# Copies of q's and k's parts spread over nine slots, and P's transposes ranked ninety places ahead

## The chip, the cores and the metric

The kernel runs on one core of a Trainium2 chip. The core has five engines with an instruction stream each: TensorE (PE in the rows, with its weight loads as PEld), VectorE (DVE), ScalarE (ACT), GpSimd (POOL) and SyncE (SP), which here only issues DMAs. The metric is the device time of one execution in microseconds (us); lower is better.

## The reference

Thresholded attention feeds two gated feed-forward blocks. What is computed, cut to what matters:

```python
# q, k, v: 4 batches x 8 heads x 576 rows x 64, float32
scores = (1 / np.sqrt(64)) * np.matmul(q, k.transpose(0, 1, 3, 2))
thresh = np.max(scores, axis=-1, keepdims=True) - tau
scores = np.where(scores >= thresh, scores, -1000000000.0)
attn = np.exp(scores - np.max(scores, axis=-1, keepdims=True))
attn = attn / (np.sum(attn, axis=-1, keepdims=True) + 1e-09)
x = np.matmul(attn, v)                      # to 2304 tokens x 512
x = (1 / (1 + np.exp(-(x @ w_gate)))) * (x @ w_val) @ w_out    # d_ff 1536
x = ((x @ w1) * (x @ w2)) @ w3 @ w_out2                        # d_ff 1024
```

## The kernel before, in words

**Three stretches.** Attention runs first, and the first block's matmuls (and, at the start, the product of w3 and w_out2) are put between attention's instructions as filler for TensorE, by `filler` and `budget`. At some 680 us attention is over, and the rest of the first block and the second block follow.

**Slots.** Attention is 16 pairs of heads (`NPAIR` = 4 for each of 4 batches), and a pair is 9 slots: four chunks of 128 query rows for each of two heads, and one slot for both heads' 64 last rows. That makes 144 slots, numbered 0 to 143 here; slot g is pair g // 9. The main loop runs over g. For a slot:

- `s_mm` (L295) makes a 128 x 576 block of scores in PSUM, as products of `qa` with `ka` and `ylz`. Two PSUM tiles take turns, so the scores of slot g + 2 wait until the mask of slot g has read its own.
- `s_max` (L317) takes the maximum on DVE, `s_exp` (L324) the exponentials on ACT into one of four `e` tiles, and `s_mask` (L331) masks on DVE.
- `s_hi` and `s_lo` (L341, L348) cut P, scaled, into a high and a low float16 part, in one of four `h16` tiles (`h` in the rows): the high part on ACT, the low part on POOL or DVE.
- `s_tr` (L362) transposes both parts with one DMA into one of five `pt` tiles. It is written two slots behind `s_mm`'s own slot.
- `pv` (L367) multiplies `pt` with V's parts on TensorE. It is written five slots behind (`LAG`).

So there are three rings: an `e` tile is free again after `s_lo`, an `h16` tile after its transpose has landed, a `pt` tile after `pv`.

**A pair's preparation.** While pair n runs, the table `ahead` places the steps that prepare pair n + 1 by slot: q's chunks are transposed on TensorE (`q_pe`), cut into a high part `xq` and a low part `yq` (`q_act`, `q_dve`), and the same for k (`xk`, `yk`). `dup` (L201) then stacks for each head `xq` over `yq` in `qa`, and `xk` over `xk` in `ka`, four SBUF to SBUF copies a head, because TensorE contracts over 128 partitions and a head has 64; `low` (L214) copies a half of `yk` into `ylz`. The loads of q, k and v for pair n + 2 stand in the same table.

**What sets the order.** Each engine runs its instructions in order. The order is set when the kernel is built, by a scheduler that takes instructions as they become ready in its own timeline, by priority; priority is the place in the program, and `tc.high_priority(offset=RING)` moves what is inside it 90 places ahead (`RING` = 90). In the kernel before, the next slots' scores, maximum, exponentials and the mask stand inside such a block. All DMAs of the kernel, the weights' loads and stores too, are issued by SP, one after the other; SP's list is therefore a queue in which an issue stands behind all issues ahead of it.

Of the kernel before, what the change touches and what calls it, by code (L numbers as in the profile page):

```python
# [8 lines left out]
F32 = mybir.dt.float32  # L9
F32R = mybir.dt.float32r  # L10
# [12 lines left out]
def kernel(  # L23
# [22 lines left out]
    nc = tc.nc  # L46
    P = 128
# [150 lines left out]
                op0=ALU.mult, op1=ALU.subtract,  # L198
            )

    def dup(pr, h):  # L201

        p = prep[pr]
        xq, yq, xk = (p[n].bitcast(F32) for n in ("xq", "yq", "xk"))
        qa = ap_.tile([P, NM], F32R, tag=f"qa{h}", name="qa", bufs=2)
        nc.sync.dma_start(qa[hsl[h]].bitcast(F32), xq[hsl[h]])
        nc.sync.dma_start(qa[hsl[1 - h]].bitcast(F32), yq[hsl[h]])
        ka = ap_.tile([P, S], F32R, tag=f"ka{h}", name="ka", bufs=2)
        for sl in hsl:
            nc.sync.dma_start(ka[sl].bitcast(F32), xk[hsl[h]])  # L210
        p.setdefault("qa", []).append(qa)
        p.setdefault("ka", []).append(ka)

    def low(pr, h):  # L214

        nc.sync.dma_start(ylz[h][hsl[h]].bitcast(F32), prep[pr]["yk"][hsl[h]].bitcast(F32))

    def low0(pr):
        low(pr, 0)

    def low1(pr):
        low(pr, 1)

    def dup0(pr):
        dup(pr, 0)

    def dup1(pr):
        dup(pr, 1)

    def k_pe(pr):  # L230
        prep[pr]["kps"] = transposed("k")
# [585 lines left out]
    l1 = None  # L817
    next(merge)
    t_pe(0, 0)
    for step in (q_pe, q_act, q_dve, k_pe, k_act, k_dve, dup0, low0, dup1, low1):  # L820
        step(0)
    load(q, 1, "q")
    load(k, 1, "k")
# [1 line left out]

    ahead = {
        0: ([], [], [], [t_pe], [q_pe]),
        1: ([q_act], [q_dve], [], [], []),
        2: ([], [v_max], ["q"], [], [k_pe]),
        3: ([k_act], [k_dve], [], [v_pe1], []),  # L830
        4: ([], [v_scale], [dup0, low0, dup1, "k"], [], []),
        5: ([], [], [], [v_pe2], []),
        6: ([], [v_mul], [], [], []),
        7: ([v_split], [], [], [], []),
        8: ([], [], [low1, "v"], [], []),
    }
# [28 lines left out]
    for g in range(G + LAG + 3):  # L865
        pr, s = divmod(g, NSL)
        steps = ahead[s] if pr + 1 < NP else ([],) * 5
        done = divmod(g - LAG, NSL)
        with tc.high_priority(offset=RING):
            if g < G:  # L870
                s_mask(g)
            if g + 1 < G:
                s_max(g + 1)
                s_exp(g + 1)
            if g + 2 < G:
                s_mm(g + 2)
        if g < G:
            s_hi(g)
        for f in steps[3]:
            f(pr + 1, g)  # L880
        if done[1] == 0 and done[0] > 0:
            x_norm(done[0] - 1)
        if g < G and g % 2 == 0 or g // (NPAIR * NSL) == 0:
            s_lo(g)
        if 0 < g <= G and not ((g - 1) % 2 == 0 or (g - 1) // (NPAIR * NSL) == 0):
            s_lo(g - 1)
        if 2 <= g < G + 2:
            s_tr(g - 2)
        for f in steps[0]:
            f(pr + 1)  # L890
        for f in steps[1]:
            f(pr + 1)
        if done[1] == 2 and done[0] > 0:
            x_act(done[0] - 1)
            if done[0] % NPAIR == 0:
                xdone[0] = done[0] // NPAIR
        filler(g, 0)
        for f in steps[2]:
            if isinstance(f, str):
                if pr + 2 < NP:  # L900
                    load(src[f], pr + 2, f)
            else:
                f(pr + 1)
        if 0 <= g - LAG < G:
            pv(g - LAG, g)
        for f in steps[4]:
            f(pr + 1)
        if done[1] == 1 and done[0] > 0:
            x_pe(done[0] - 1, g)
        filler(g, 1)  # L910
# [270 lines left out]
```

## Time and profile before

| | |
|---|---|
| median of 3 runs | 1116.5 us (1116.19 to 1119.25) |
| span of the profiled execution | 1115.6 us |
| TensorE busy | 1008.3 us, 90% of the span |
| VectorE busy | 774.8 us, 69% |
| GpSimd busy | 676.3 us, 61% |
| ScalarE busy | 627.6 us, 56% |

The profile gives the profiled execution's time as the span from its first to its last instruction, 1115.6 us, 0.9 us below the median of the runs. Busy shares are means over the three stretches, which have different limits. A wait is put down to what ended it.

### The profile page before, as it was taken

The numbers are of one execution on the slowest core, as the hardware profiler recorded it, in microseconds if no ns is written. First come the engines' busy times: TensorE is split into PE (matmuls) and PEld (weight loads), VectorE is DVE, ScalarE is ACT, GpSimd is POOL, SyncE is SP. The second block draws the span as 40 slices with busy tenths as digits, with TensorE's granted clock in tenths as the row PEclk, the third lists the DMA queues.
The fourth block names the chain that finished last, engine by engine and source line by source line (L and its number), as shares of the span: only waits on it lengthen the run. The fifth ranks groups of instructions, "written<-read, shape, count | busy, mean of one in ns | idle before, by whom it ended". The sixth has DMA issues, their size and how long they took to land. (4 is left out here: it accounts for less than half of the span.)

```text
span 1115.6 us, 20323 instructions
## 1 busy us (share of the span) xinstructions
PE 1008.3 (90%) x6960; PEld 884.9 (79%) x6960; DVE 774.8 (69%) x1380; ACT 627.6 (56%) x1245; POOL 676.3 (61%) x577
## 2 busy tenths in 40 slices
PE   2598956898987999999999998999999999999997
PEld 2477845676765787777877888999999989988996
DVE  6978687888897767767877645776767644652741
ACT  4868898767777676567667644554442322331321
POOL 3755475587888586678677855677664643462530
PEclk9789967999988999999999999999999999999999
DMA  8999999999999999898988864677558826844922
GB/s 227 245 274 211 225 218 173 241 280 264 270 286 235 200 209 210 211 210 180 201 198 184 161 140 153 215 234 250 184 193 293 256 80 229 282 131 128 325 69 63
DMA packets 322422, 232.57 MB, mean 208 GB/s; under 512 B 225296, under 2 KB 253968, under 8 KB 322320
## 3 DMA queue, kind: packets, MB, share of 16 engines
q1 hardware_dynamic: 322320, 231.28, 80.9%
q8 instruction: 55, 0.90, 0.3%
q14 instruction: 47, 0.39, 0.1%
HBM read 133.17 MB, written 30.93 MB: 147 GB/s over the span
## 5 line engine op out<-in xcount | busy, mean ns | idle before, releaser
L358 POOL TENSOR_TENSOR h<-e,h 128x576 f16<-128x576 f32 x90 | 120.1, 1336 | 39.9 <-ACT e L355 29.7
L327 ACT ACTIVATE e<-ps_s,nm 128x576 f32<-128x576 f32 x144 | 106.1, 737 | 51.0 <-DVE nm L321 49.8
L336 DVE SCALAR_TENSOR_TENSOR e<-ps_s,th,e 128x576 f32<-128x576 f32 x144 | 116.2, 811 | 20.3 <-ACT th L328 12.5
L63 PEld LDWEIGHTS <-pt 128*128 128x128 f16 x2240 | 82.1, 101 | 58.8 <-DMA pt<-h 32.3
L321 DVE TENSOR_REDUCE nm<-ps_s 128x1 f32<-128x576 f32 x144 | 106.3, 751 | 28.9 <-PE ps_s L63 19.9
L344 ACT ACTIVATE h<-e 128x576 f16<-128x576 f32 x144 | 97.0, 678 | 28.3 <-DVE e L336 14.8
L63 PE MATMUL ps_s<-ka,qa 128*128 128x288 f32 x256 | 67.5, 351 | 42.2 <-DVE e L336 31.4
L63 PE MATMUL ps_h<-xl,gh 128*128 128x512 f32 (+1 forms) x240 | 94.7, 395 | 6.3 <-POOL xl L469 2.8
L63 PE MATMUL ps_h<-xl,vh 128*128 128x512 f32 (+1 forms) x240 | 92.7, 386 | 2.4 <-ACT th L685 1.3
L63 PE MATMUL ps_h<-xh,gl 128*128 128x512 f32 (+1 forms) x240 | 91.3, 380 | 3.3 <-POOL gl L469 3.3
L469 POOL TENSOR_TENSOR gl<-wg,gh 128x512 fp32r<-128x512 f32 x42 | 55.4, 1319 | 61.4 <-ACT gh L468 61.4
L63 PE MATMUL ps_y<-wm,abh 128*128 128x512 f32 x288 | 91.6, 390 | 0.2 <-DVE wm L469 0.2
L63 PE MATMUL ps_h<-xh,vl 128*128 128x512 f32 (+1 forms) x240 | 90.2, 376 | 1.6 <-POOL vl L469 1.6
L63 PE MATMUL ps_o<-gvl,oh 128*128 128x512 f32 (+1 forms) x240 | 90.4, 376 | 1.0 <-DVE XR L718 1.0
L63 PE MATMUL ps_h<-xh,gh 128*128 128x512 f32 (+1 forms) x240 | 90.8, 378 | 0.0
L63 PE MATMUL ps_h<-xh,vh 128*128 128x512 f32 (+1 forms) x240 | 90.2, 376 | 0.0
L63 PE MATMUL ps_o<-gvh,ol 128*128 128x512 f32 (+1 forms) x240 | 88.5, 369 | 0.3 <-POOL ol L469 0.3
L63 PE MATMUL ps_o<-gvh,oh 128*128 128x512 f32 (+1 forms) x240 | 88.2, 368 | 0.0
L63 PE MATMUL u<-vh,pt 128*128 128x64 f16 x640 | 62.6, 200 | 27.6 <-DMA pt<-h 27.2
L63 PEld LDWEIGHTS ps_s<-ka,qa 128*128 128x128 f32 x256 | 45.6, 210 | 50.5 <-DVE e L336 36.5
L360 DVE SCALAR_TENSOR_TENSOR h<-e,h 128x576 f16<-128x576 f32 x54 | 61.4, 1137 | 23.2 <-ACT h L344 22.8
L469 POOL TENSOR_TENSOR ol<-wo,oh 128x512 fp32r<-128x512 f32 x42 | 55.7, 1330 | 24.0 <-ACT oh L468 23.9
(198 smaller groups left out, 3025.2 us busy)
## 6 DMA issues: line engine op xcount, KB each, us to landing
wc<-sc_c SPq DMA_DIRECT2D x168, 256.0 KB, 3.2
sc_c<-wc SPq DMA_DIRECT2D x56, 256.0 KB, 2.9
XR<-in_moe_w_out_dram SPq DMA_DIRECT2D x20, 512.0 KB, 5.0
ka<-xk SPq DMA_DIRECT2D x64, 144.0 KB, 3.3
wg<-sc_g SPq DMA_DIRECT2D x36, 256.0 KB, 3.1
wv<-sc_v SPq DMA_DIRECT2D x36, 256.0 KB, 3.1
wo<-sc_o SPq DMA_DIRECT2D x36, 256.0 KB, 3.2
XR<-in_moe_w_dram SPq DMA_DIRECT2D x16, 512.0 KB, 5.0
```

Of the source, the lines that this page charges most:

```text
L63: nc.tensor.matmul(out_, lhsT, rhs, start=first, stop=last)
L321: nc.vector.tensor_reduce(nm, x["ps"], axis=AX.X, op=ALU.max, negate=True)
L327: nc.scalar.activation(e, x["ps"], AF.Exp, bias=x["nm"])
L336: nc.vector.scalar_tensor_tensor(x["e"], x["ps"], x["th"], x["e"], op0=ALU.is_ge, op1=ALU.mult, accum_out=prep[pr]["sum"][:, s:s + 1],)
L344: nc.scalar.activation(x["h16"][:, 0:S], x["e"], AF.Copy, scale=PSC)
L358: nc.gpsimd.tensor_tensor(lo, e, hi, op=ALU.subtract)
L360: nc.vector.scalar_tensor_tensor(lo, e, PSC, hi, op0=ALU.mult, op1=ALU.subtract)
L469: (lo_eng or nc.gpsimd).tensor_tensor(lo, x, hi.bitcast(F32), op=ALU.subtract)
```

## The change

`dup` becomes two steps, one for q and one for k, so that the copies of a pair stand in slots 2, 3, 4 and 5 instead of three quarters of them in slot 4; the copies themselves are the same. q's load moves from slot 2 to slot 1, k's from slot 4 to slot 6. And `s_tr` moves into a block of high priority, 90 places ahead of its place in the program.

```diff
-    def dup(pr, h):
-        p = prep[pr]
-        xq, yq, xk = (p[n].bitcast(F32) for n in ("xq", "yq", "xk"))
+    def dup_q(pr, h):
+        p = prep[pr]
         qa = ap_.tile([P, NM], F32R, tag=f"qa{h}", name="qa", bufs=2)
-        nc.sync.dma_start(qa[hsl[h]].bitcast(F32), xq[hsl[h]])
-        nc.sync.dma_start(qa[hsl[1 - h]].bitcast(F32), yq[hsl[h]])
+        for sl, n in ((hsl[h], "xq"), (hsl[1 - h], "yq")):
+            nc.sync.dma_start(qa[sl].bitcast(F32), p[n].bitcast(F32)[hsl[h]])
+        p.setdefault("qa", []).append(qa)
+
+    def dup_k(pr, h):
+        p = prep[pr]
         ka = ap_.tile([P, S], F32R, tag=f"ka{h}", name="ka", bufs=2)
         for sl in hsl:
-            nc.sync.dma_start(ka[sl].bitcast(F32), xk[hsl[h]])
+            nc.sync.dma_start(ka[sl].bitcast(F32), p["xk"].bitcast(F32)[hsl[h]])
...
     ahead = {
         0: ([], [], [], [t_pe], [q_pe]),
-        1: ([q_act], [q_dve], [], [], []),
-        2: ([], [v_max], ["q"], [], [k_pe]),
-        3: ([k_act], [k_dve], [], [v_pe1], []),
-        4: ([], [v_scale], [dup0, low0, dup1, "k"], [], []),
-        5: ([], [], [], [v_pe2], []),
-        6: ([], [v_mul], [], [], []),
+        1: ([q_act], [q_dve], ["q"], [], []),
+        2: ([], [v_max], [dupq0], [], [k_pe]),
+        3: ([k_act], [k_dve], [dupq1], [v_pe1], []),
+        4: ([], [v_scale], [dupk0], [], []),
+        5: ([], [], [low0, dupk1], [v_pe2], []),
+        6: ([], [v_mul], ["k"], [], []),
         7: ([v_split], [], [], [], []),
         8: ([], [], [low1, "v"], [], []),
     }
...
         if 2 <= g < G + 2:
-            s_tr(g - 2)
+            with tc.high_priority(offset=RING):
+                s_tr(g - 2)
```

The scheduler then sets another order on every engine. Three places show it. In the rows a line number is that of the kernel they come from: s_tr's DMA is L364 before and L358 of the change, the copies are L206, L207, L210 and L216 before and L205, L212 and L217 of the change, L440 and L434 load raw weights, L639 and L633 store cast ones.

SP's list up to the transpose of slot 57 (pt<-h_3745), before:

```order
L206 DMA qa<-xq 64x512
L207 DMA qa<-yq 64x512
L210 DMA ka<-xk 64x576 x2
L216 DMA ylz_95<-yk 64x576
L206 DMA qa<-xq 64x512
L207 DMA qa<-yq 64x512
L210 DMA ka<-xk 64x576 x2
L145 DMA km<-in_k_dram 128x4x64 x2
L149 DMA tails<-in_k_dram 64x2x64
L639 DMA sc_o_130<-wo 128x512
L440 DMA XR<-in_moe_w_gate_dram 128x4x128
L364 DMA_TRANSPOSE pt<-h_3745 128x9x128
```

SP's list around the transpose of slot 57 (pt<-h_3748), of the change:

```order
L205 DMA qa<-xq 64x512
L205 DMA qa<-yq 64x512
L633 DMA sc_o_129<-wo 128x512
L434 DMA XR<-in_moe_w_gate_dram 128x4x128
L205 DMA qa<-xq 64x512
L205 DMA qa<-yq 64x512
L358 DMA_TRANSPOSE pt<-h_3748 128x9x128
L633 DMA sc_g_107<-wg 128x512
L434 DMA XR<-in_moe_w_val_dram 128x4x128
L633 DMA sc_v_119<-wv 128x512
L434 DMA XR<-in_moe_w_out_dram 128x512
L212 DMA ka<-xk 64x576 x2
```

Of the twelve issues of the preparation that stood in one row ahead of this transpose, four are left ahead of it, the copies of qa; ka, ylz and k's load now stand behind it, and six issues of weights that stood ahead do too.

SP's list from the transpose of slot 24 (pt<-h_1850) to that of slot 25 (pt<-h_1888), before:

```order
L364 DMA_TRANSPOSE pt<-h_1850 128x9x128
L216 DMA ylz_96<-yk 64x576
L135 DMA vnat<-in_v_dram 64x2x64
L440 DMA XR<-in_moe_w_val_dram 128x4x128
L145 DMA vnat<-in_v_dram 128x256
L639 DMA sc_g_100<-wg 128x512
L145 DMA vnat<-in_v_dram 128x256
L149 DMA vnat<-in_v_dram 64x2x64
L364 DMA_TRANSPOSE pt<-h_1888 128x9x128
```

The last twelve rows up to the transpose of slot 25 in SP's list, of the change (five more rows stand between them and the transpose of slot 24):

```order
L282 DMA vsh<-vh 64x2x256
L434 DMA XR<-in_moe_w_out_dram 128x512
L283 DMA vsh<-vh 64x2x256
L135 DMA vnat<-in_v_dram 64x2x64
L145 DMA vnat<-in_v_dram 128x256 x2
L633 DMA sc_v_112<-wv 128x512
L149 DMA vnat<-in_v_dram 64x2x64
L145 DMA qm<-in_q_dram 128x4x64
L205 DMA qa<-xq 64x512
L205 DMA qa<-yq 64x512
L205 DMA qa<-xq 64x512
L358 DMA_TRANSPOSE pt<-h_1888 128x9x128
```

The transpose of slot 25 had seven issues between it and the one before it, and now has seventeen, three copies of qa among them.

TensorE's list up to the first rows of pv of slot 50, before; the rows with ka are the first half of the scores of slot 58:

```order
L156 MATMUL ps_t<-ident,km 128x128 x4
L63 MATMUL ps_h<-xl,vh 128x512
L63 MATMUL ps_s_88<-ka,qa 128x288 x2
L63 MATMUL ps_h<-xh,vl 128x512
L63 MATMUL ps_h<-xh,vh 128x512
L63 MATMUL ps_h<-xl,vh 128x512
L63 MATMUL ps_h<-xh,vl 128x512
L63 MATMUL ps_h<-xh,vh 128x512
L63 LDWEIGHTS pt
L63 MATMUL u<-vh,pt 128x64
```

TensorE's list at the end of pv of slot 49 and the start of pv of slot 50, of the change; the rows with ka and ylz are the scores of slot 54:

```order
L63 LDWEIGHTS pt
L63 MATMUL u<-vsh,pt 128x64
L63 MATMUL ps_s_88<-ka,qa 128x288 x2
L63 LDWEIGHTS pt
L63 MATMUL u<-vsh,pt 128x64
L63 LDWEIGHTS pt
L63 MATMUL u<-vh,pt 128x64
L63 MATMUL ps_s_88<-ylz_95,qa 128x288 x2
```

pv of slot 50 stood behind the scores' start of slot 58, and now stands behind that of slot 54: TensorE's list holds fewer matmuls between a slot's scores and its pv. Between the last score product of slot 50 and pv of slot 50 the list holds 108 matmuls of 512 columns, 32 of 288, 112 of 64 and 16 of 128 before, and 54, 16, 90 and 7 in the change.

## Rows read from the trace of the kernel before

**Rows 1.** Windows: stretch and its us, busy us of each engine, clock, DMA share, GB/s.

```profile
core 0: us, PE busy (x) PEld busy (x) DVE busy (x) ACT busy (x) POOL busy (x), PEclk, DMA share, GB/s
37.00:200.00 163.00, 128.31 (x1115) 108.73 (x1115) 130.26 (x260) 127.94 (x252) 94.41 (x76) 0.84 1.00 222
200.00:400.00 200.00, 173.94 (x1335) 142.00 (x1336) 170.28 (x314) 146.88 (x290) 149.59 (x122) 0.94 1.06 253
400.00:690.00 290.00, 277.84 (x2208) 226.80 (x2207) 201.07 (x369) 186.18 (x372) 201.50 (x171) 0.99 0.83 185
690.00:1116.00 426.00, 418.38 (x2270) 399.74 (x2268) 246.37 (x381) 145.65 (x293) 217.00 (x190) 1.00 0.60 196
```

**Rows 2.** Waits from 37 to 200 us: us in total, times, longest.

```profile
PE u L63 <- DMA pt<-h: 23.8, 15, 4.3
```

**Rows 3.** Waits from 200 to 400 us.

```profile
PE ps_s L63 <- DVE e L336: 11.1, 5, 5.2
...
ACT h L344 <- DMA pt<-h: 6.7, 7, 2.1
...
PE ps_h L63 <- POOL gl L469: 3.3, 2, 2.0
```

**Rows 4.** Timeline of SP from 338 us: start, us, the issue.

```profile
338.02 0.59 SPq L216 DMA_DIRECT2D ylz<-yk  x1
...
341.33 1.31 SPq L145 DMA_DIRECT2D km<-in_k_dram  x2
342.68 0.63 SPq L149 DMA_DIRECT2D tails<-in_k_dram  x1
343.42 4.28 SPq L364 DMA_TRANSPOSE pt<-h  x2
```

**Rows 5.** Timeline of POOL: the low part of slot 66.

```profile
324.76 1.29 POOL L358 TENSOR_TENSOR h<-e,h 128x576 f16<-128x576 f32 x1
```

**Rows 6.** Timeline of PE: four waits, idle time and its releaser in brackets.

```profile
51.30 0.24 PE L63 MATMUL u<-vh,pt 128*128 128x64 f16 x1 [3.01 <-DMA pt<-h]
...
311.36 0.85 PE L63 MATMUL ps_s<-ka,qa 128*128 128x288 f32 x2 [2.26 <-DVE e L336]
...
352.87 0.20 PE L63 MATMUL u<-vh,pt 128*128 128x64 f16 x1 [1.66 <-DMA pt<-h]
...
358.62 0.85 PE L63 MATMUL ps_s<-ka,qa 128*128 128x288 f32 x2 [5.17 <-DVE e L336]
```

**Rows 7.** Windows around the last three of these waits, columns as in rows 1.

```profile
300.00:347.00 47.00, 41.99 (x313) 34.09 (x313) 41.23 (x75) 33.70 (x66) 35.56 (x28) 0.93 1.12 261
347.00:381.00 34.00, 24.38 (x231) 20.40 (x230) 26.72 (x49) 24.17 (x49) 24.98 (x21) 0.85 1.03 227
```

**Rows 8.** Line L364 from 200 to 380 us: issue ns, then us to landing.

```profile
L364 SPq DMA_TRANSPOSE pt<-h x36: 1261/1654/3447, 200.9 to 372.2; - x36
...
DMA to landing us min/median/max: 3.2/5.3/7.8
```

**Rows 9.** Page, costliest groups: a slot's steps, count, busy us, mean ns, idle before.

```profile
L358 POOL TENSOR_TENSOR h<-e,h 128x576 f16<-128x576 f32 x90 | 120.1, 1336 | 39.9 <-ACT e L355 29.7
L327 ACT ACTIVATE e<-ps_s,nm 128x576 f32<-128x576 f32 x144 | 106.1, 737 | 51.0 <-DVE nm L321 49.8
L336 DVE SCALAR_TENSOR_TENSOR e<-ps_s,th,e 128x576 f32<-128x576 f32 x144 | 116.2, 811 | 20.3 <-ACT th L328 12.5
...
L321 DVE TENSOR_REDUCE nm<-ps_s 128x1 f32<-128x576 f32 x144 | 106.3, 751 | 28.9 <-PE ps_s L63 19.9
L344 ACT ACTIVATE h<-e 128x576 f16<-128x576 f32 x144 | 97.0, 678 | 28.3 <-DVE e L336 14.8
...
L360 DVE SCALAR_TENSOR_TENSOR h<-e,h 128x576 f16<-128x576 f32 x54 | 61.4, 1137 | 23.2 <-ACT h L344 22.8
```

**Rows 10.** Timeline of PE: first and last of twelve matmuls in a row.

```profile
345.79 0.39 PE L63 MATMUL ps_h<-xl,vh 128*128 128x512 f32 x1
...
348.30 0.40 PE L63 MATMUL ps_h<-xh,vh 128*128 128x512 f32 x1
```

More of the change, by code (lines that the diff above doesn't have):

```diff
@@ L199, in q_dve @@
             )
-    def dup(pr, h):
+    def dup_q(pr, h):
         p = prep[pr]
-        xq, yq, xk = (p[n].bitcast(F32) for n in ("xq", "yq", "xk"))
         qa = ap_.tile([P, NM], F32R, tag=f"qa{h}", name="qa", bufs=2)
-        nc.sync.dma_start(qa[hsl[h]].bitcast(F32), xq[hsl[h]])
-        nc.sync.dma_start(qa[hsl[1 - h]].bitcast(F32), yq[hsl[h]])
+        for sl, n in ((hsl[h], "xq"), (hsl[1 - h], "yq")):
[3 more added lines that the diff above has]
+        p = prep[pr]
         ka = ap_.tile([P, S], F32R, tag=f"ka{h}", name="ka", bufs=2)
         for sl in hsl:
-            nc.sync.dma_start(ka[sl].bitcast(F32), xk[hsl[h]])
-        p.setdefault("qa", []).append(qa)
+            nc.sync.dma_start(ka[sl].bitcast(F32), p["xk"].bitcast(F32)[hsl[h]])
         p.setdefault("ka", []).append(ka)
@@ L216, in low, with per_head @@
         nc.sync.dma_start(ylz[h][hsl[h]].bitcast(F32), prep[pr]["yk"][hsl[h]].bitcast(F32))
[L218 to L228, printed above, removed]
+    def per_head(f):
+        return [lambda pr, h=h: f(pr, h) for h in range(2)]
+    (dupq0, dupq1), (dupk0, dupk1), (low0, low1) = (per_head(f) for f in (dup_q, dup_k, low))
     def k_pe(pr):
@@ L819 @@
     t_pe(0, 0)
-    for step in (q_pe, q_act, q_dve, k_pe, k_act, k_dve, dup0, low0, dup1, low1):
+    for step in (q_pe, q_act, q_dve, k_pe, k_act, k_dve, dupq0, dupk0, low0, dupq1, dupk1, low1):
         step(0)
```

## The prediction

> **What bounds the kernel now.** I read the windows first, then the waits stretch by stretch, then the timelines of the engines around the longest waits. The windows [rows 1] show where time is to be had. From 690 us on TensorE is busy for 418.4 of 426 us, and the change alters no order there: nothing to win or lose. From 400 to 690 us it is busy for 277.8 of 290 us. From 200 to 400 us it stands still for 200 - 173.9 = 26 us, and from 37 to 200 us for 163 - 128.3 = 35 us, at granted clocks of 0.94 and 0.84 of full speed. So the change can only work on these 61 us and on the slow clock beside them. In both stretches the DMA share is 1.00 or more.
>
> In the first stretch 23.8 us of the idle time are 15 waits of a pv for its transpose [rows 2]. In the second the longest item is the scores' wait for a mask, 11.1 us in 5 times; there ACT's high part waits 7 times for an h16 tile that a transpose has not yet given back, and waits for weights' parts come after that, 3.3 us [rows 3].
>
> The timelines tell why. The low part of slot 66 was ready at 324.76 + 1.29 = 326.05 us [rows 5], and its transpose was issued at 343.42 us, 17.4 us later [rows 4]. SP was not waiting in the last part of that: from 338.02 us to 343.31 us its rows follow each other without a hole, and all of them are copies and loads of the next pair's preparation. With the transpose late, the h16 tile came back late, the high part of slot 70 with it, then the low part, then the `e` tile of slot 74, then its exponentials and mask. TensorE's wait of 5.17 us at 358.62 us is the end of that chain, and the 1.66 us at 352.87 us are slot 68's transpose in the same jam. The 2.26 us at 311.36 us have the same cause one pair earlier, in slot 57 [rows 6].
>
> **Part 1, the copies.** Nothing is added or removed. The order lists of the change show four copies ahead of slot 57's transpose where twelve issues of the preparation and more stood, and between slots 36 and 96 no other transpose but slot 43's stands behind more than nine issues, where seven stood behind eleven or more. Part 2, the rank of the transposes, works in the same place, so I cost them together: a transpose of slots 46 to 95 stands some six weight issues and up to twelve others further ahead.
>
> *Term A, the jams of slots 57 and 66.* Idle time: 2.26 + 1.66 + 5.17 = 9.1 us [rows 6]. The clock fell to its lower level, 1.2 GHz, behind them: the two windows have 0.93 and 0.85, which is (1 - 0.93) x 2 x 47 = 6.6 us and (1 - 0.85) x 2 x 34 = 10.2 us at half speed; TensorE was busy for 42.0 of 47 and 24.4 of 34 us, and loses half of the busy part, 2.9 + 3.7 = 6.6 us [rows 7]. Together 15.7 us if both jams go away wholly. The lower bound is nothing: SP's rows are gapless, so what leaves the place ahead of a transpose is issued behind it and delays something else. I take half, -8 us, because the two items that move back, ka and weights, have a pair's length or two filler units to land, whereas a transpose had none.
>
> *Term B, from 37 to 200 us.* The wait of 3.01 us at 51.30 us is for the transpose of slot 3 [rows 6], and in the list of before four copies of qa and a load stood ahead of it that now stand behind: 5 issues at about 0.6 us [rows 4] are 3 us. The other waits of this stretch are for transposes whose place hardly moves. Bounds 0 and 23.8 us [rows 2]; I take -3 us.
>
> *Term C, the transpose of slot 25.* It now has seventeen issues between it and the one before, against seven. Ten issues by 0.6 us [rows 4] are 6 us at most, nothing at least, since some of them went out while SP waited anyway. It is one place, nearer to nothing because the copies of qa there no longer stand ahead of slots 28 to 30: +2 us.
>
> *Term D, less look-ahead on TensorE.* The scheduler thinks the transposes early and therefore places a pv mostly four to six scores behind its own instead of six to eight, in slots 36 to 88. For slot 50 the list between scores and pv now holds 54 matmuls of 512 columns, 16 of 288, 90 of 64 and 7 of 128. Twelve matmuls of 512 took (348.30 - 345.79) / 11 = 0.228 us each [rows 10]; by columns (an estimate) that is 12.3 + 2.1 + 2.6 + 0.4 = 17.4 us, where before it was some 33 us. In that time must fit: maximum 0.75, exponentials 0.74, mask 0.81, high part 0.68, low part 1.14 to 1.34 [rows 9], issue to landing 5.3 [rows 8], together 9.5 us, and some hand-over between engines, say 10. That leaves 7.4 us for standing in SP's queue. Slot 66 stood 17.4 us, of which the copies' jam alone, from 338.02 to 343.31, was 5.3 [rows 4, 5]; six weight issues and the rest less at 0.6 us take away as much again, so 17.4 - 5.3 - 3.6 = 8.5 us would be left in a bad slot and less in an ordinary one. I take an occasional wait, +2 us; bounds 0 and the second rival's price.
>
> Moving q's load a slot earlier and k's two later costs nothing: each is used a pair later, and it lies beside some five slots of TensorE's work; without that cover k's would show as a wait of the transposes ps_t.
>
> *Sum.* -8 - 3 + 2 + 2 = -7 us on the profiled 1115.6 us, 1108.6 us; the runs' median lies 0.9 us above the span, so 1109.5 us.
>
> **The rivals.**
>
> *Nothing comes of it (1113.2 to 1119.9 us).* SP's rows are gapless [rows 4] and the DMA share is 1.06 from 200 to 400 us [rows 1]: the same issues in another order take the same time, and every place that a transpose wins a weight or a copy loses. PE would wait for POOL's parts of the weights instead of for masks. Against it: those waits are 3.3 us now [rows 3], so weights have some room. A rule speaks for this rival: the Trainium skill, Perfetto Trace Analysis, section What "DMA-bound" means, says that a kernel can be bound by its DMA engines or by the sequencer that issues, seen as a track solid with DMA slices, and that larger descriptors are then what helps; an order alone would give nothing. By that rule terms A and B would be zero and the sum some 1120 us; the trace agrees that the track is solid in places, but TensorE still worked for 87% of that stretch, so it is no pure bound. The centre of this rival, by the rows, is 1116.5 us.
>
> *Slower (over 1119.9 us): pv too early on TensorE.* The place is slots 36 to 88, 53 slots; a wait also helps the next four or so, so it could fall some 12 times. If a transpose still stands 9 us in SP's queue instead of 7.4, that is 12 x 1.6 = 19 us, less A and B (11): 1116.5 + 8 = 1124.5 us. It decides from about 8.5 us of queue on, where 12 x 1.1 = 13 us eat up the gain. For it speaks that slots 57 to 66 land in 5.3 us in the middle and up to 7.8 [rows 8]; against it, that the h16 ring no longer holds up the high part.
>
> *A larger gain.* A whole, and half of the waits of rows 2: -15.7 - 12 = 1089 us; I count as this anything under 1102 us.
>
> **How the numbers follow.** 0.3% of 1116.5 us is 3.3 us, about what a measurement of this kernel can tell from no change. I give the forecast (1102 to 1113.2 us) 0.42, the larger gain 0.12, nothing 0.22, slower 0.24. Faster is then 0.54, same 0.22, slower 0.24. The time is the forecast's, 1109.5 us. The range leaves out a tenth at each end: the lower part of the larger gain below 1097, and the upper part of the second rival above 1124.
>
> **What would show it.** In the changed profile the waits of the scores for the mask of DVE between 300 and 370 us should be gone or under 2 us, and the clock there near 1.00 (A). The wait at slot 3's pv should be near nothing (B). The pv of slot 25 should wait up to some us (C). Between 200 and 400 us the waits of pv for transposes may grow from 2 us; by more than 15 us, the second rival is right (D). If the scores' waits for masks go and waits of ps_h for weights' parts come in their place, the first rival is. The prediction is wrong if the order on SP was not what made the transposes late, for example if their low parts came late from POOL.

## The result and the profile after

The changed kernel is slower: 1128.9 us median (1120.06 to 1132.4, 14 runs) against 1119.5 us of the kernel before on the same chip (1116.19 to 1124.37, 14 runs), ratio 1.0075 with a 95% interval of 1.0059 to 1.0091, that is some 8.4 us (the two medians alone differ by 9.4 us). The profiled execution has a span of 1126.7 us, 11.1 us more than before's.

The windows of the changed kernel, columns as in [rows 1]:

```profile
37.00:200.00 163.00, 125.51 (x1033) 105.83 (x1034) 127.22 (x250) 124.29 (x244) 93.21 (x76) 0.84 0.97 222
200.00:400.00 200.00, 171.26 (x1328) 138.06 (x1327) 162.22 (x304) 140.67 (x276) 141.79 (x115) 0.95 1.01 242
400.00:690.00 290.00, 276.45 (x2229) 225.66 (x2228) 207.69 (x382) 192.08 (x386) 204.43 (x176) 0.99 0.88 192
690.00:1127.00 437.00, 429.50 (x2327) 409.96 (x2325) 250.75 (x391) 148.51 (x300) 219.32 (x191) 0.99 0.60 192
```

TensorE is busy for 2.8 us less in the first stretch and for 2.7 us less in the second, at about the same clock: the two places where something was to be won lost. The waits say where. From 37 to 200 us (us in total, times, longest):

```profile
PE u L63 <- DMA pt<-h: 17.8, 15, 3.1
PE ps_s L63 <- DVE e L330: 17.0, 11, 6.2
```

From 200 to 400 us:

```profile
PE u L63 <- DMA pt<-h: 8.1, 7, 3.0
PE ps_s L63 <- DVE e L330: 5.4, 5, 2.5
PE ps_h L63 <- ACT th L679: 3.4, 1, 3.4
PE ps_t L156 <- DVE t L450: 3.1, 1, 3.1
```

Up to 200 us the waits of pv for transposes fell by 6.0 us [rows 2]. Part of that is the edge of the window: slot 0's wait, 4.3 us, ended at 37.27 us before, inside it, and that of the change, 2.6 us, at 35.83 us, ahead of it; with both counted the fall is 23.8 - (17.8 + 2.6) = 3.4 us. The scores' waits for masks, 8.6 us in 5 times before, doubled. From 200 to 400 us the waits for masks halved [rows 3] as forecast, and three others came or grew: pv for transposes (2.2 us in 2 times before, 1.66 us of it in [rows 6]), a product of the first block that waits for an activation on ACT, and q's transposition on TensorE, which waits for a weight cast on DVE.

**Where in the kernel.** The windows cut by the clock on the wall; a late kernel shows other work in them. So I also took from each trace the moment at which TensorE's matmuls had covered as many columns as in the first profile of before at 37, 140, 200, 300, 400 and 600 us. The table has how much longer each kernel took from one such moment to the next than the mean of two profiles of before (the second is one of the experiments below); the column "all" goes from the start to 680 us. Kinds of matmuls differ in us per column, so a us or two between neighbours says nothing. The two profiles of before are 0.0 to 1.0 us from their mean, but single profiles scatter more: nine profiles have the lists of before up to 140 us (before's own two and the seven with late parts only), and they lie from -0.9 to +4.0 us in the first column. One cell of less than some 4 us shows nothing by itself; what several profiles of the same lists share counts.

```
kernel                 37-140 140-200 200-300 300-400 400-600   all   measured ratio (95%)
the change               +0.4    +4.2    +7.1    -2.6    +2.1  +10.6  1.0075 (1.0059 to 1.0091)
the change again         +0.1    +4.4    +6.6    -4.8    +0.3   +6.1  1.0059 (1.0033 to 1.0086)
before again             +0.9    +0.3     0.0    -0.1    -1.0   +0.6  0.9979 (0.9957 to 1.0001)
e1_copies                +5.5    +1.1    +2.2    -2.0    -1.3   +4.5  1.0050 (1.0027 to 1.0073)
e1_rank                  +3.0    -0.6    +6.5    -4.6    -0.4   +3.7  1.0095 (1.0061 to 1.0128)
e1_rank_late             +6.3    -1.4   +14.4    -9.2    +2.2  +11.9  1.0113 (1.0084 to 1.0142)
e1_rank45                +2.4    +1.9    +5.2    -9.5    +0.2   -0.2  1.0002 (0.9982 to 1.0023)
e2_copies_late           +4.0    -0.6    +1.9    -1.3    -3.5   +0.3  0.9999 (0.9978 to 1.0020)
e2_both_late             +1.2    -3.3    +8.4    -5.1    -1.4   -1.6  1.0009 (0.9987 to 1.0030)
e2_both_early            -0.1    +2.8    +2.5    -5.8    +0.3   -1.8  1.0009 (0.9987 to 1.0031)
e2_rank45_late           +2.6    -3.1    +4.2    -4.5    +1.0   +0.1  0.9988 (0.9962 to 1.0013)
e3_no_rank36_92          +0.7    +2.6    +0.4    -1.4    +1.1   +2.9  1.0031 (1.0007 to 1.0054)
e3_after_loads_act       -9.4    -0.2    +8.6    -6.3    -0.8   +3.4  1.0021 (0.9990 to 1.0053)
e3_before_loads_act      -2.4    +0.6    +2.8    +1.7    -7.2   +2.3  1.0028 (1.0005 to 1.0051)
e4_late45                +1.4    -0.7   +11.9    -8.7    +5.8   +9.9  1.0065 (1.0035 to 1.0096)
e4_early45               -0.7    +2.5    +5.4    -0.6    +0.8   +7.5  1.0074 (1.0053 to 1.0096)
e4_late45_rank45         +1.1    -1.1    +5.8    +1.3    +0.9   +7.9  1.0059 (1.0039 to 1.0080)
e5_rank60                +2.2    -1.6    +2.5     0.0    +1.2   +5.7  1.0038 (1.0018 to 1.0058)
e5_copies54_rank60       +2.3    +0.1    +1.9    -3.2    +0.9   +1.5  1.0004 (0.9988 to 1.0020)
```

The change loses some 4 us between 140 and 200 us and some 7 us between 200 and 300 us, and wins 3 to 5 us back between 300 and 400 us. The two kernels with loads on ACT reach the first moment 13.1 and 8.5 us late, all others within 0.6 us.

**140 to 200 us: masks behind the weights' work.** DVE's timeline of the changed kernel (L330 are the masks, of slots 26, 27 and 28 here; L444 and L450 casts of the first block's weights; xl is a low part in the first block):

```profile
145.69 0.81 DVE L330 SCALAR_TENSOR_TENSOR e<-ps_s,th,e 128x576 f32<-128x576 f32 x1
...
149.80 3.22 DVE L463 TENSOR_TENSOR xl<-XR,xh 128x512 fp32r<-128x512 f32 x1
152.95 0.68 DVE L444 TENSOR_SCALAR ps_c<-XR 128x512 uint32<-128x512 uint32 x1
153.73 0.69 DVE L450 SCALAR_TENSOR_TENSOR t<-XR,ps_c 128x512 uint32<-128x512 uint32 x1
154.34 0.68 DVE L233 TENSOR_TENSOR yk<-ps_t,xk 128x512 fp32r<-128x512 f32 x1
154.94 0.68 DVE L444 TENSOR_SCALAR ps_c<-XR 128x512 uint32<-128x512 uint32 x1
155.53 0.81 DVE L330 SCALAR_TENSOR_TENSOR e<-ps_s,th,e 128x576 f32<-128x576 f32 x1
...
156.86 0.81 DVE L330 SCALAR_TENSOR_TENSOR e<-ps_s,th,e 128x576 f32<-128x576 f32 x1
```

The same in the second profile of before, masks L336:

```profile
147.81 0.81 DVE L336 SCALAR_TENSOR_TENSOR e<-ps_s,th,e 128x576 f32<-128x576 f32 x1
...
150.47 0.81 DVE L336 SCALAR_TENSOR_TENSOR e<-ps_s,th,e 128x576 f32<-128x576 f32 x1
...
152.59 1.18 DVE L469 TENSOR_TENSOR xl<-XR,xh 128x512 fp32r<-128x512 f32 x1
...
155.67 0.81 DVE L336 SCALAR_TENSOR_TENSOR e<-ps_s,th,e 128x576 f32<-128x576 f32 x1
```

Before, the mask of slot 27 starts 2.7 us after that of slot 26; in the change twelve other instructions stand between them (two of them the maxima of slots 27 and 28) and it starts 9.8 us after. TensorE's scores wait for it at the first of these rows; the other two are the second profile of the change, and before's wait in its second profile, for slot 28:

```profile
156.40 0.85 PE L63 MATMUL ps_s<-ka,qa 128*128 128x288 f32 x2 [6.17 <-DVE e L330]
```

```profile
156.15 0.85 PE L63 MATMUL ps_s<-ka,qa 128*128 128x288 f32 x2 [6.45 <-DVE e L330]
```

```profile
156.54 0.85 PE L63 MATMUL ps_s<-ka,qa 128*128 128x288 f32 x2 [3.38 <-DVE e L336]
```

This wait is not the whole loss. The stretch from the second of the moments to the third, before and then in the change, columns as in [rows 1]:

```profile
139.94:199.51 59.57, 39.15 (x384) 33.27 (x383) 47.72 (x98) 48.68 (x100) 35.09 (x29) 0.74 0.97 196
141.49:205.53 64.04, 42.24 (x403) 35.47 (x401) 50.75 (x101) 51.52 (x105) 38.35 (x33) 0.68 0.87 194
```

TensorE stands still for 20.4 us before and 21.8 us in the change (20.9 and 21.9 us in the second profiles): the longer wait for a mask is nearly made up by shorter ones. Some 3 of the 4.5 us between the two rows are busy time, 39.2 us before and 42.2 us in the change, at a granted clock of 0.74 and of 0.68 (0.71 in the second profile), that is with more of it at the lower of the two levels, 1.2 GHz. How much of it is the clock and how much the 19 matmuls more, of smaller kinds, is not separated.

**200 to 300 us: pv too close behind its scores.** TensorE's timeline of the changed kernel at pv of slot 42, and SP's and POOL's at slots 42, 66 and 72:

```profile
211.16 0.20 PE L63 MATMUL u<-vh,pt 128*128 128x64 f16 x1 [0.37 <-DMA pt<-h]
...
214.71 0.23 PE L63 MATMUL u<-vh,pt 128*128 128x64 f16 x1 [2.97 <-DMA pt<-h]
```

```profile
209.62 1.30 SPq L358 DMA_TRANSPOSE pt<-h  x1
...
342.00 1.32 SPq L358 DMA_TRANSPOSE pt<-h  x1
...
367.81 0.63 SPq L149 DMA_DIRECT2D vnat<-in_v_dram  x1
376.08 1.34 SPq L358 DMA_TRANSPOSE pt<-h  x1
```

```profile
329.68 1.29 POOL L352 TENSOR_TENSOR h<-e,h 128x576 f16<-128x576 f32 x1
...
373.54 1.27 POOL L463 TENSOR_TENSOR gl<-wg,gh 128x512 fp32r<-128x512 f32 x1
374.77 1.28 POOL L352 TENSOR_TENSOR h<-e,h 128x576 f16<-128x576 f32 x1
```

The transpose of slot 42 was issued at 209.62 us and TensorE stood at its pv from 211.74 to 214.71 us. The second profile has the wait again (2.29 us at 213.38 us). In both profiles of before no pv waits for a transpose for over 0.4 us between 200 and 350 us.

**300 to 400 us: other waits in the old ones' place.** The transpose of slot 66 is issued 342.00 - (329.68 + 1.29) = 11.0 us after its low part instead of 17.4 [rows 4, 5], and the waits that answer to the last two of [rows 6] are gone (0.46 us are left of the 5.17); the one at slot 3 is 1.59 us instead of 3.01. The wait of 2.26 us at 311.36 us, of the scores of slot 67 for the mask of slot 65, is not gone: it is the first of these rows, and 2.50 us in the second profile. The other three have come:

```profile
326.03 0.53 PE L63 MATMUL ps_s<-ka,qa 128*128 128x288 f32 x2 [2.49 <-DVE e L330]
...
352.19 0.79 PE L63 MATMUL ps_h<-xl,vh 128*128 128x512 f32 x1 [3.38 <-ACT th L679]
...
370.82 0.66 PE L401 MATMUL ps_x<-ident,xn 128*128 128x128 f32 x4 [1.48 <-DVE xn L386]
...
374.60 0.70 PE L156 MATMUL ps_t<-ident,qm 128*128 128x128 f32 x4 [3.13 <-DVE t L450]
```

That is 10.5 us against 9.1 us. Why the mask of slot 65 is still late shows on DVE: its threshold is ready on ACT at 322.35 us, TensorE stands from 323.54 us, and DVE's list puts a maximum, parts of q and k and a weight cast ahead of it. The weight cast and the mask:

```profile
324.15 0.67 DVE L450 SCALAR_TENSOR_TENSOR t<-XR,ps_c 128x512 uint32<-128x512 uint32 x1
...
325.15 0.82 DVE L330 SCALAR_TENSOR_TENSOR e<-ps_s,th,e 128x576 f32<-128x576 f32 x1
```

And SP itself now stands: nothing is issued from 368.44 to 376.08 us, because the transpose of slot 72 heads its list and the low part it needs is done at 376.05 us, behind gl and other parts of the first block on POOL. The second profile shows the same stand (4.9 us).

### The profile page after: what moved, and what is told of

It reads as the page before. It is cut to its first block, busy times and chain, and to the rows that moved or that the text cites. A ratio compares the mean times of both kernels' runs of the same rounds, so it can differ in the third digit from the quotient of the medians.

```text
span 1126.7 us, 20305 instructions
## 1 busy us (share of the span) xinstructions
PE 1013.5 (90%) x6960; PEld 887.9 (79%) x6960; DVE 774.4 (69%) x1380; ACT 626.3 (56%) x1245; POOL 672.5 (60%) x577
## 5 line engine op out<-in xcount | busy, mean ns | idle before, releaser
L352 POOL TENSOR_TENSOR h<-e,h 128x576 f16<-128x576 f32 x90 | 116.2, 1296 | 54.1 <-ACT e L349 39.6
L330 DVE SCALAR_TENSOR_TENSOR e<-ps_s,th,e 128x576 f32<-128x576 f32 x144 | 115.9, 811 | 23.6 <-ACT th L322 15.1
L463 POOL TENSOR_TENSOR vl<-wv,vh 128x512 fp32r<-128x512 f32 x43 | 58.2, 1354 | 17.2 <-ACT vh L462 17.1
```

Of the source, the lines that this page charges most:

```text
L330: nc.vector.scalar_tensor_tensor(x["e"], x["ps"], x["th"], x["e"], op0=ALU.is_ge, op1=ALU.mult, accum_out=prep[pr]["sum"][:, s:s + 1],)
L352: nc.gpsimd.tensor_tensor(lo, e, hi, op=ALU.subtract)
L463: (lo_eng or nc.gpsimd).tensor_tensor(lo, x, hi.bitcast(F32), op=ALU.subtract)
```

## The experiments

All are timed against the kernel before; the profile of each is in the table above.

**First set: which part.** Three explanations run through the expectations: START (the lists around the first block's start, at 140 to 165 us, cost the time), LOOK-AHEAD (pv stands too close behind its scores from 200 us on) and SCATTER (any new order moves the time by some us, tied to no part). Of a pair's ten copies the table of before has nine in slot 4, the halves of `yk` counted. Against the change, `e1_copies` drops the rank:

```diff
-            with tc.high_priority(offset=RING):
-                s_tr(g - 2)
+            s_tr(g - 2)
```

> Only the copies and loads moved; the transposes keep their old rank. Three theories. START: the loss of the change comes from DVE, ACT and POOL taking the first block's weight work ahead of attention's steps of slots 25 to 28 (6.2 us of wait and 3.4 us more of slow clock, about +5 us); this kernel's list on DVE has nine instructions of other work between the masks of slots 26 and 27 where the change has ten and the kernel before one, so START expects the wait at some 156 us again, and about +5 us on the kernel before. LOOK-AHEAD: the loss comes from pv standing 4 to 6 scores behind in slots 46 to 88; here it is 6 or 7, so it expects that the 7 us between 200 and 260 us come back and, if START is nothing by itself, about the time of before or 2 to 8 us less. SCATTER: any new order of this schedule moves the time by some us either way with no tie to a part; it expects no agreement with either.

Measured: 1.0050. Slower by some 5.6 us without any rank; the wait of START is there, 5.06 us at 159.38 us, but by the table most of the loss lies ahead of 140 us, with a wait of 3.83 us for an xn at 124.87 us in it (`e2_copies_late`, with before's lists there, has +4.0 us in the same column). And the wait that the forecast put down to the copies is still there, longer than before's and two slots earlier:

```profile
362.33 0.85 PE L63 MATMUL ps_s<-ka,qa 128*128 128x288 f32 x2 [5.97 <-DVE e L330]
```

Its mask stands behind a low part that took 6.83 us on DVE (1.14 us in the mean before), while POOL worked without a hole; DVE's row, then POOL's:

```profile
351.11 6.83 DVE L354 SCALAR_TENSOR_TENSOR h<-e,h 128x576 f16<-128x576 f32 x1 [1.17 <-ACT h L338]
```

```profile
351.07 1.29 POOL L352 TENSOR_TENSOR h<-e,h 128x576 f16<-128x576 f32 x1
352.32 1.29 POOL L463 TENSOR_TENSOR gvl<-gr,gvh 128x512 fp32r<-128x512 f32 x1
353.57 1.30 POOL L352 TENSOR_TENSOR h<-e,h 128x576 f16<-128x576 f32 x1
354.81 2.51 POOL L463 TENSOR_TENSOR xl<-XR,xh 128x512 fp32r<-128x512 f32 x2
359.28 1.65 POOL L463 TENSOR_TENSOR gvl<-gr,gvh 128x512 fp32r<-128x512 f32 x1 [1.96 <-ACT gvh L462]
```

`e1_rank` is the kernel before with the rank alone:

```diff
-            s_tr(g - 2)
+            with tc.high_priority(offset=RING):
+                s_tr(g - 2)
```

> Only the rank of the transposes moved; copies and loads stand where they were. START: eight other instructions stand between DVE's masks of slots 26 and 27, so the wait there comes again, +5 us. LOOK-AHEAD: pv is placed 5 to 6 scores behind in slots 46 to 72 and 4 to 5 in slots 74 to 82, so most of the loss of 200 to 400 us comes too: together about the +9 us of the change, or more, since the copies still jam transposes 49 and 58 (14 issues ahead of each). SCATTER: no tie to either.

Measured: 1.0095 (7 runs, 1121.66 to 1131.27 us; the profiled one is the fastest of them). It loses 6.5 us between 200 and 300 us, as LOOK-AHEAD said; START's loss is not in the table (-0.6 us), though its lists have eight instructions between the masks and its wait there is 4.13 us.

`e1_rank_late` and `e1_rank45` change the rank in the change:

```diff
-            with tc.high_priority(offset=RING):
+            with tc.high_priority(offset=RING if g >= 36 else 0):   # e1_rank_late
+            with tc.high_priority(offset=45):                       # e1_rank45
```

> The change, but the transposes are ranked ahead only from slot 34 on. Up to slot 36 its lists are those of the kernel with the copies alone, from slot 50 on those of the change. START: as the copies alone up to 200 us (wait at 156 us again). LOOK-AHEAD: the loss from 200 to 400 us is that of the change. Both together: about +9 us, the change's own. If the rank of the early transposes is what costs, it is +4 or less.

> The change with the transposes ranked 45 places ahead in place of 90. Its pv stand 5 to 7 scores behind in slots 46 to 88, half-way between the change and the copies alone; START is the same (ten other instructions between the masks of slots 26 and 27). LOOK-AHEAD: half of the 7 us lost between 200 and 260 us comes back, +5 us on the kernel before; START alone: +9 us as the change.

Measured: 1.0113 and 1.0002. The first is the slowest of all: 14.4 us lost between 200 and 300 us, 5.35 us of them in one wait of a pv for its transpose at 235.90 us, and 9.2 us won back. The second had lost 9.5 us from 37 to 300 us, nearly as much as the change (11.7 us), and won all of it back by 400 us, where it was expected at +5 or +9 us.

**Second set: early or late half.** The old table and the old rank up to about slot 35 (or from there on), `ahead_old` being the table of before (g is the main loop's, and the transpose written in it is slot g - 2's):

```diff
-        steps = ahead[s] if pr + 1 < NP else ([],) * 5
+        steps = (ahead if pr >= 4 else ahead_old)[s] if pr + 1 < NP else ([],) * 5
...
-            with tc.high_priority(offset=RING):
+            with tc.high_priority(offset=RING if g >= 36 else 0):
```

`e2_both_late` is this; `e2_copies_late` has no rank; `e2_rank45_late` has 45 for `RING`; `e2_both_early` has `pr < 4` and `g < 36`.

> The lists of before up to about slot 25, then copies and loads spread from pair 5's on (written from slot 36 on); transposes keep their old rank. In every run so far that had either part from the start, the same TensorE work was reached 6 to 11 us later at 160 us, whatever came behind. START: without the new order around the first block's start this loss does not occur, and what is left is the copies' own worth, the jams at slots 57 and 66: -4 to -8 us on the kernel before. SCATTER (each new order costs or gains some us by chance, also behind 200 us): anything from -5 to +8 us. LOOK-AHEAD says little here, since pv stands 6 to 8 scores behind as before: about -4 us.

> As the run with the late copies, and the transposes ranked 90 ahead from slot 36 on: the change without its first 36 slots. START: the change's +8.4 us less the 6 us lost up to 165 us, that is about +2 us on the kernel before. LOOK-AHEAD: pv stands 4 to 6 scores behind from slot 37 to 74, so this is slower than the run with the late copies by about the 7 us by which the rank made the change's late part slower than the copies alone: some +1 to +3 us as well. SCATTER: no tie.

> The change's lists up to slot 37, then the rules of before for copies, loads and transposes. START: the whole 6 us up to 165 us are lost and nothing is won back, since the jams at slots 57 and 66 are as before: +5 to +6 us on the kernel before, and at equal TensorE work the distance stays flat from 200 to 680 us. If the loss is made behind 200 us by the late transposes' rank, this is within 2 us of before.

> As the run with the late copies, and the transposes ranked 45 places ahead from slot 36 on. The change with rank 45 throughout ended level with the kernel before although it had lost 6.6 us by 160 us. START: without that loss it is 5 to 7 us faster than the kernel before, the best so far. LOOK-AHEAD: a little slower than the late copies alone, -2 to -4 us. SCATTER: no tie, level or slower.

Measured: 0.9999, 1.0009, 1.0009, 0.9988: all four level with before. START as a plain sum falls: the early half alone shows its loss in the profile (+2.8 us from 140 to 200 us) and not in the time. The late half loses 8.4 us between 200 and 300 us and wins 5.1 us of them back by 400 us. Together they cost 8.4 us.

**Third set: SP's queue.** `e3_after_again` is the change itself. `e3_no_rank36_92` has

```diff
-            with tc.high_priority(offset=RING):
+            with tc.high_priority(offset=RING if not 36 <= g < 92 else 0):
```

and the last two issue the loads of q, k and v from ACT, in the change and in the kernel before:

```diff
     def load(src, pr, nm):
...
-            nc.sync.dma_start(
+            nc.scalar.dma_start(
```

> The change itself, unaltered, for a second profile and more times. Two trace comparisons of single executions can differ by some us at equal TensorE work although the lists are the same (three kernels with the lists of before stood 0, 1.4 and 5.1 us behind it at 200 us). START says that the loss up to 165 us is in the order and comes again: 4 to 6 us behind before at 160 us, with a wait of about 6 us near 156 us. LOOK-AHEAD says that waits of pv for transposes near 215 to 245 us come again, 5 us in sum. Both expect the time 7 to 10 us above before. If the 6 us of SP standing at the transpose of slot 72 near 376 us come again, that place is part of the order too; if not, it was chance.

> The change with the transposes' old rank in slots 36 to 91; copies, loads and the first 36 slots as in the change. START and LOOK-AHEAD as sums of parts: the early part alone cost 0 in its own run, the copies alone 5.6 us, so this should lie between, 0 to +6 us on before, that is 3 to 8 us faster than the change, by what the short distance between scores and pv costs from slot 50 on. SP-BOUND (SP issues for 0.9 of the time from 100 to 560 us, so every time it stands with its in-order list at an issue that is not ready is lost for good): the transposes stand further behind, SP stands less at them, and the time is near before's as well; the two part in what SP's row shows: SP-BOUND expects fewer us of idle SP between 100 and 500 us than the change's 29.

> The change with the loads of q, k and v issued by ACT instead of SP: about 110 of SP's issues between 37 and 620 us, some 75 to 90 us of its 513 us, go to another queue. SP-BOUND: SP is then busy for 0.75 instead of 0.9, catches up behind every stand, and the change's 8.4 us come back wholly: at most before's time, perhaps 5 us less. START and LOOK-AHEAD, where the loss lies on DVE, POOL and in the order of pv: still +5 to +9 us on before, more if ACT's own work is held up by the issues.

> The kernel before with the same loads issued by ACT: the control. SP-BOUND: faster too, by 3 to 8 us, since its own jams at slots 57 and 66 are SP's queue. START and LOOK-AHEAD say nothing of it; if both kernels with ACT's loads are level, the change's loss needs a full SP queue; if they differ by 8 us again, it does not.

Measured: 1.0059 for the change again, with every wait named above at its place to within a few us: these losses come again with the order. Without the rank from 36 to 91: 1.0031, and +0.4 us between 200 and 300 us instead of +7: that loss comes with the rank. With the loads on ACT: 1.0021 (0.9990 to 1.0053) for the change and 1.0028 (1.0005 to 1.0051) for the kernel before. SP then issues for 440 and 424 us from 37 to 620 us instead of 513 and 509 us (the sum of its rows, with its waits for semaphores), and neither is faster than before. But the test paid for the relief at the start: TensorE comes to the first moment of the table 13.1 us later in the one and 8.5 us later in the other. From 140 to 680 us the kernel before with its loads on ACT takes 3.8 us less than with them on SP, and the change 0.3 us less than before, where with all issues on SP it takes 10.5 and 6.3 us more. The two with loads on ACT are level with each other, which by what was expected speaks for a loss that needs a full queue; but of the change's two losses only the first is gone (-0.2 us from 140 to 200 us) and the second stands (+8.6 us). These are single profiles; whether SP's queue bounds the kernel behind its start stays open, and so does whether the change's loss needs a full queue (0.9990 to 1.0053 holds almost all of it).

**Fourth set: the split at slot 45.** As the second set, with `pr >= 5` and `g >= 45` (`e4_late45`; with 45 for `RING` `e4_late45_rank45`), or `pr < 5` and `g < 45` (`e4_early45`), and the kernel before itself.

> The kernel before, unaltered, for a second profile and as a null: a ratio of 1 within 0.25%. If the jams are in its order, the waits of about 5 us near 358 us and about 2 us near 311 us come again. If START is right, there is no wait over 4 us near 156 us, and between 140 and 160 us of the first profile's TensorE work it loses nothing against it.

> Before's rules up to slot 44, then the change's (copies and loads spread, transposes ranked 90 ahead). START and LOOK-AHEAD at slots 36 to 45 both say that this has the gain of the missing jams without either loss: -3 to -6 us on before. If the short distance between scores and pv costs all the way to slot 88, or if the gain was never there, 0 to +4 us.

> The change's rules up to slot 44, then before's. START plus LOOK-AHEAD at slots 36 to 45: both losses (some 5 and 5 us) and, with before's late part, the jams as well: +5 to +10 us on before. If it is level like the early part up to slot 36, then no loss of the change up to 250 us lasts, and what makes the change slow is behind slot 45.

> As the late change from slot 45 on, with rank 45 instead of 90, so that pv stands 5 to 7 scores behind in place of 4 to 6. The likeliest of all to beat the kernel before: -4 to -7 us if the late part gains; level if it does not.

Measured: 0.9979 (0.9957 to 1.0001) for the kernel before against itself, so some 0.2% can be chance. Its waits come again where they were, 2.26 us, 1.69 us and 4.98 us:

```profile
314.90 0.85 PE L63 MATMUL ps_s<-ka,qa 128*128 128x288 f32 x2 [2.26 <-DVE e L336]
...
356.26 0.20 PE L63 MATMUL u<-vh,pt 128*128 128x64 f16 x1 [1.69 <-DMA pt<-h]
...
361.82 0.85 PE L63 MATMUL ps_s<-ka,qa 128*128 128x288 f32 x2 [4.98 <-DVE e L336]
```

The others miss: `e4_late45` was expected at -3 to -6 us, or up to +4, and has 1.0065, with rank 45 1.0059. It loses 11.9 us between 200 and 300 us although its lists up to about slot 42 are before's, and only 1.7 us of that are pv's waits for transposes; the scores' waits for masks are 5.7 us and one for ylz is 3.1 us. All idle time in that stretch is 17.4 us against 11.5 and 10.5 us in the two profiles of before, about half of the loss; the rest is busy time at a granted clock of 0.91 against 0.97 and 0.95. Distance to pv alone doesn't explain it. `e4_early45`, 1.0074, was as START and LOOK-AHEAD in sum had it.

**Fifth set: does the gain stand.** `e5_rank60` is `e1_rank` with `offset=RING if g >= 60 else 0`; `e5_copies54_rank60` has the new table from `pr >= 6` on as well.

> The kernel before with one change, the transposes ranked 90 ahead from slot 60 on; up to about 290 us its lists are those of before. GAIN-STANDS (the rank breaks the chain behind the wait of 5 us near 358 us, whatever came ahead): nothing lost up to 300 us, 3 to 6 us won between 300 and 400 us, total -3 to -6 us on before. GAIN-IS-RETURN (what the ranked kernels win there is only what they had lost between 200 and 300 us, because the limit behind it lies elsewhere): level or slower, 0 to +5 us, with a loss of its own where the rank begins.

> As the last, with copies and loads spread from slot 54 on as well. GAIN-STANDS: -3 to -7 us on before. GAIN-IS-RETURN: 0 to +5 us.

Measured: 1.0038 and 1.0004, as GAIN-IS-RETURN had it. In `e5_rank60` the wait of 5 us is gone, and nothing is won between 300 and 400 us, where these waits stand instead:

```profile
PE u L63 <- DMA pt<-h: 2.8, 2, 2.3
PE ps_x L407 <- DVE xn L392: 2.2, 1, 2.2
PE ps_s L63 <- DMA ylz<-yk: 1.8, 1, 1.8
```

But both theories had nothing lost up to 300 us, and `e5_rank60` loses 2.2 - 1.6 + 2.5 = 3.1 us there by the table, although its lists up to 303 us are those of before but for one exchange (a transpose and a copy of ylz, pv of slot 24 and the next scores, near 147 us). So 3 us in one profile can come without the order that is tested, and its 1.0038 is no clean price of the rank from slot 60 on.

## Why the prediction was wrong

1109.5 us was forecast, 1128.9 us came, beyond the range and past the second rival (1124.5 us). 3.0 us of the difference are the kernel before, which has 1119.5 us in these runs and had 1116.5 us in those that the prediction went by; the rest is a loss, 8.4 us by the ratio, where a gain of 7 us was forecast. By its own steps:

**Term A, -8 us.** The order on SP did what was read from the lists: the transpose of slot 57 is issued 7.5 us after its low part instead of 20.3, that of slot 66 11.0 us instead of 17.4. The failing steps come after it. The first is the chain: two of the three waits went, but the one put down to slot 57 stayed, 2.49 us instead of 2.26, because the mask of slot 65 stands behind other work on DVE. The second is that idle time which goes is won. Between 300 and 400 us the two profiles of the change show -2.6 and -4.8 us, and the clock from 347 to 381 us is still 0.85, as in [rows 7]. The chain on which I rested the wait of 5.17 us was one of several that end near the same place. The copies alone leave 5.97 us there, through DVE; the rank alone from slot 60 on takes it away and wins 0.0 us, and a transpose, a copy of ylz and an xn are waited for instead; and of the kernels with all issues on SP that win there five win what they had lost since 37 us to within 1.2 us, and the others less.

**Term B, -3 us.** The wait at slot 3 shrank by 1.4 us and all waits for transposes up to 200 us by 3.4 us, slot 0's counted on both sides, but up to 140 us the change is level (+0.4 and +0.1 us): the scores' waits for masks up to 140 us grew from 0.6 to 5.6 us. The step that failed is that a shorter wait of pv is won.

**Term C, +2 us.** The wait at pv of slot 25 is 2.07 us at 161.13 us, as forecast. Two things end together there: the seventeen issues fill SP from 145.47 to 157.71 us with no hole over 0.6 us, and the low part, ready at 140.24 us before, is now ready at 157.08 us, late on POOL. SP's rows, then POOL's (the low parts of slots 25 and 26):

```profile
157.11 0.60 SPq L205 DMA_DIRECT2D qa<-xq  x1
157.81 2.73 SPq L358 DMA_TRANSPOSE pt<-h  x2
```

```profile
155.79 2.54 POOL L352 TENSOR_TENSOR h<-e,h 128x576 f16<-128x576 f32 x2
```

With the one mended, the other would still have held the transpose to within 0.7 us; a low part late from POOL is the case that the prediction named as its own undoing, and here it shares the place.

**Term D, +2 us.** The mechanism was right for the change and the size wrong: +7.1 and +6.6 us between 200 and 300 us. The step that failed is the choice of slot 50 for the whole stretch. By the same count of matmuls the lists of the change hold 10.4 us between the scores and pv of slot 42 (27 of 512 columns, 10 of 288, 91 of 64, 6 of 128) where before held 16.3. Against the 10 us that a slot's steps need, that leaves 0.4 us for SP's queue, not 7.4, and the waits fall at slots 42, 43 and 46. The shown waits for transposes, 8.1 and 6.0 us from 200 to 300 us, are about this size in the change; all idle time there grew by 5.9 and 3.5 us, since other waits fell. From 200 to 400 us pv's waits grew by 5.9 us, not by the 15 us that were to show the second rival: the time passed its price by other losses beside this one. And in other ranked kernels (`e4_late45`) the same loss came by other waits. The queue was misread as well: the 8.5 us left for slot 66 were already more than the 7.4 us that the list left, and it stood 11.0 us; by SP's lists one weight issue less stands ahead of its transpose, not six.

**What had no term, +4.2 and +4.4 us.** The scheduler also moved DVE's list: twelve instructions between two masks at the start of the first block. I read SP's and TensorE's lists and not DVE's, on which the scores wait as well. The five profiles of kernels that have both parts with rank 90 in the first slots, and all issues on SP, show a loss here (+2.5 to +4.4 us), and those with before's early lists do not (-3.3 to +0.3 us). That the wait for the mask makes all of it is not shown: the idle time of the stretch grew by only 1.2 us, and the kernels with one part alone have such a wait too (5.06 and 4.13 us) with +1.1 and -0.6 us.

These sum, in means of the two profiles, to 0.2 + 4.3 + 6.9 - 3.7 + 1.2 = 8.9 us; measured were 8.4 and 6.6 us. **Still open** is why the parts don't add up: each half at slot 36 is level, both together are not, and the split at slot 45 costs 7 to 8 us either way. Of the fourteen other new orders that kept all issues on SP, six are level with before within their intervals, eight are slower, none is faster. This fits SCATTER, and no experiment here replaced it by a rule. No version was found that beats the kernel before; 0.9988 (0.9962 to 1.0013) is the best.

## What to carry to other kernels

Where a scheduler sets the order, a priority is a change to every engine's list: compare all of them at the tightest slot, not at a typical one, before costing one queue. A wait at the end of a long chain is worth its length only if no other chain ends just behind it; a second profile and a kernel with one part show that sooner than a timeline does. And in such a kernel a null run and a handful of neutral reorderings tell what an order is worth by chance: here from level to 1.1% slower. An experiment that moves work to another engine has to be read by stretch as well: the loads on ACT cost 8.5 us at the start of the kernel before, which can hide what they gave behind it.

## What the runs showed of the hardware

A DVE instruction can take as long as POOL keeps working. The low part h on DVE took 6.83 us from 351.11 us while POOL ran five instructions without a hole up to 357.32 us, and DVE's ended 0.62 us after the last of them. The xl of 3.22 us at 149.80 us (1.18 us in before) ended 0.55 us after POOL's gl at 152.47 us. In the changed kernel even a small one did, beside POOL at work from 301.17 to 305.74 us (2.88 us at the same place in the second profile; of the sixteen of its kind in the changed kernel eight took under 0.7 us):

```profile
302.89 2.89 DVE L382 TENSOR_SCALAR rs<-sum 128x9 f32<-128x9 f32 x1
```

The Trainium skill, SBUF — State Buffer, section SBUF: two separate sides, has the rule: a DVE instruction in a 2-port mode or with two SBUF inputs shares a port pair with GpSimd's, and whichever starts first holds it for its whole instruction. The trace agrees that one waits for the other, and goes further: the DVE instruction waited not for one of POOL's but for five in a row.

Order, more than chance, sets where this kernel's long waits fall: in two profiles each of the two kernels the same waits came again, 2.26 and 2.26 us, 1.66 and 1.69 us, 5.17 and 4.98 us before, 6.17 and 6.45 us, 2.97 and 2.29 us after.
